# A Fourier mixer and an ELU feed-forward on one core: batch 1's twelve weight groups by three products in place of four

## The chip, the cores and the metric

The kernel runs on one core of one Trainium2 chip. The metric is the device time of one execution in microseconds (us); where several runs are shown, their median is taken. TensorE (PE in the profile) multiplies matrices, VectorE (DVE), ScalarE (ACT) and GpSimd (POOL) work element by element, and SyncE (SP) issues most of the transfers.

## The reference

```python
X = rfft(x, axis=1)                       # x: 8 batches x 3008 positions x 256
Yr = Xr @ w_r - Xi @ w_i + b_r
Yi = Xr @ w_i + Xi @ w_r + b_i
Y = sign(Y) * max(|Y| - 0.01, 0)          # real and imaginary part apart
y = irfft(Y, n=3008, axis=1)
h = y.reshape(24064, 256) @ moe_w_in      # 256 x 2048
g = where(h > 0, h, exp(min(h, 0)) - 1)
out = g @ moe_w_out                       # 2048 x 256
```

## The kernel before, in words

The transform over 3008 = 47 x 64 positions is done as small matrix products in five kinds of units. **A** transforms over 47 positions, **X** over 64 and leaves the spectrum in the tile `XT` with the real part (c=0) beside the imaginary part (c=1), for two halves of the 256 features (dt=0 and 1). **M** applies the weights `w_r` and `w_i` to 128 frequencies at a time, adds the bias and shrinks by 0.01. **B** and **Y** transform back; Y's result is `yT`, the input of the feed-forward. Between A and X, M and B, B and Y the data are turned through DRAM or SBUF by transfers: `DA` into `Z` (`load_Z`, line 223), `Y` into `Yx` (`turn_Y`, line 434), `DB` into `Bs` (`load_Bs`, line 476).

The feed-forward is a chain of 376 steps, 47 for each batch, in the main loop (line 1317). Step i multiplies 512 positions by 256 of the 2048 inner columns (`front`, line 1096: four matmuls of 512 columns into two banks of a pool of four, `hps`), turns the result into the ELU and multiplies that of step i-2 by `moe_w_out` (`back`, line 1174: eight matmuls of 256 columns). The ELU is exp on ScalarE, a clamp, and one last instruction on VectorE for each half (`finish_elu`, line 1153), which is issued a step later and frees the `hps` banks that `front` takes two steps later. The clamp (`elu`, line 1165) is done in one of three ways: on GpSimd (two instructions, line 1169), on VectorE (one of 128x1024, line 1171), or not at all, where ScalarE takes a Relu ahead of the exp (lines 1128 and 1133; steps with an M unit).

`plan(b)` (line 1222) lays the units of the next batch over the 47 steps of batch b: `f0[t]` holds what is issued ahead of step t's `front`, `f1[t]` what is issued behind it. Each engine runs its instructions in the order in which they are issued. For batch 1, prepared while batch 0 is worked on, the units start at step 10 (`FILL`): X0 to X7 in steps 10 to 17, M in 18 to 23, 25, 26, 28, 29, 31 and 32, B in 24, 27, 30 and 33 to 35, then the A and Y units. The six transfers that fill `Z` for batch 1 are issued in step 5: first three for the slots 0 to 7, then three for the slots 8 to 31. X unit (g, dt) reads the slots 8g to 8g+7.

There are two forms of M. Batches 0 and 1 use `m_group` (line 283): four matmuls of 128x512, one VectorE addition of the bias (line 302), and on GpSimd a clip (line 314) and a subtraction (line 315). Batches 2 to 7 use three real products (lines 317 to 350): six matmuls of 128x256, (Xr+Xi) w_r, Xi times -(w_i + w_r), and Xr times (w_i - w_r), two VectorE additions (lines 340, 341), and on GpSimd a further bias addition (line 346), the clip (349) and the subtraction (350). These need `sum_XT` (line 255; three GpSimd additions for each dt, in tiles `XS` and `busy`) and the weights as `three_weights` (line 272) makes them, five GpSimd instructions in steps 47 to 50.

The M groups of `m_group` take two banks from the pool that the X and B units use (`psF`, one tile of two banks), the three products two single banks of `psM`; changing between the two pools makes the new one wait for what the old one still holds. A B unit reads what `turn_Y` has moved of both M groups with its number; `turn_Y` for the last pair of batch 1 issues two of its four transfers from GpSimd's queue (line 438).

Of the kernel before, what the change touches and what calls it, by code (L numbers as in the profile page):

```python
# [8 lines left out]
ALU = mybir.AluOpType  # L9
# [20 lines left out]
def kernel(  # L30
# [11 lines left out]
    nc = tc.nc  # L42
    P = nc.NUM_PARTITIONS

    B, S, D = x.shape
# [5 lines left out]
    LAM = 0.01  # L51
# [44 lines left out]
    PER = S * NPAIR // TB  # L96
# [8 lines left out]
    Y_of = {}  # L105
# [17 lines left out]
    def unit_ps(name, alone):  # L123
        if alone:
            return pre2.tile([P, 2, 512], F32, name=name, tag="pre2")
        return last_banks("psF").tile([P, 2, 512], F32, name=name, tag="fps")
# [100 lines left out]
        nc.sync.dma_start(Z[a:P:4, s0:s1, :], dv[rows * a : rows * a + rows, s0:s1, :])  # L227

    def unit_X(b, u, alone=False, on_dve=False, apart=False):
        g, dt = (u // 2, u % 2) if b == 1 else (u % 4, u // 4)  # L230
        if u == 0:
            XT_of[b] = xtp.tile([P, 2, 2, K1 * N2], BF16, name="XT", tag="XT")
        XT = XT_of[b]
        if apart:
            psv = [t[:].rearrange("p (k j) -> p k j", j=P) for t in two_banks(pre1, "mps1")]
        else:
            ps = unit_ps("xps", alone)
            psv = [ps[:].rearrange("p a (k j) -> p (a k) j", j=P)]
        nk = 8 // len(psv)
        for kk in range(8):  # L240
            k = 8 * g + kk
            nc.tensor.matmul(  # L242
                psv[kk // nk][:, kk % nk, 0 : 4 * K1],
                lhsT=Z[:, k, dt * P : dt * P + P],
                rhs=M2[:, k].rearrange("p c m -> p (c m)"), start=True, stop=True,
            )
        for h, v in enumerate(psv):
            k0 = 8 * g + nk * h
            evac(
                XT[:, dt].rearrange("p c (m s) -> p c m s", s=NS)[:, :, :, k0 : k0 + nk],  # L250
                v[:, :, 0 : 4 * K1].rearrange("p k (c m) -> p c m k", c=2),
                on_dve and not h if apart else on_dve,
            )
# [24 lines left out]
            b_r_, b_i_ = (bias_bc[:, D * k : D * k + D] for k in range(2))  # L278
            nc.gpsimd.tensor_tensor(b_i_, b_i_, b_r_, ALU.subtract)

    mps_of = {}

    def m_group(b, q, i, ps, biased=False):
        XT = XT_of[b]
        o = (2 * q + i) * P
# [21 lines left out]
        return yb, clip  # L307

    def unit_M(b, q, i):
        if b == 1:  # L310
            if i == 0:
                mps_of[q] = unit_ps("mps", False)
            yb, clip = m_group(b, q, i, mps_of[q][:, i, :])
            nc.gpsimd.tensor_scalar(clip[:], yb, LAM, -LAM, ALU.min, ALU.max)
            nc.gpsimd.tensor_tensor(Y_of[b, q][:, i, :], yb, clip[:], ALU.subtract)
            return
        XT, o = XT_of[b], (2 * q + i) * P
        if i == 0:
            Y_of[b, q] = wk4.tile([P, 2, 2 * D], BF16, name="Y", tag="Y")
        ps, k1 = (  # L320
            last_banks("psM").tile([P, 2 * D], F32, name="mps", tag="mps") for _ in range(2)
        )
        ch, oc = divmod(o, 512)
        r, s = wcat_r, wcat_s
        todo = [
            (k1[:, 0:D], None, r[:, :, 0:D]),
            (ps[:, 0:D], XT[:, :, 1, o : o + P], s[:, :, 0:D]),
            (ps[:, D : 2 * D], XT[:, :, 0, o : o + P], s[:, :, D : 2 * D]),
        ]
        if o == 0 and b > 3:  # L330
            todo.append(todo.pop(0))
        for out_, lhs, w in todo:
            for dt in range(2):
                nc.tensor.matmul(  # L334
                    out_, lhsT=lhs[:, dt] if lhs is not None else sum_of(dt, ch)[:, oc : oc + P],
                    rhs=w[:, dt, :], start=(dt == 0), stop=(dt == 1),
                )
        yb = wk3.tile([P, 2 * D], F32, name="yb", tag="yb")
        clip = wk2.tile([P, 2 * D], F32, name="clip", tag="clip")
        nc.vector.tensor_tensor(yb[:, D : 2 * D], k1[:, 0:D], bias_bc[:, 0:D], ALU.add)  # L340
        nc.vector.tensor_tensor(  # L341
            yb[:].rearrange("p (c d) -> p c d", c=2),
            ps[:].rearrange("p (c d) -> p c d", c=2),
            yb[:, D : 2 * D].unsqueeze(1).to_broadcast([P, 2, D]), ALU.add,
        )
        nc.gpsimd.tensor_tensor(  # L346
            yb[:, D : 2 * D], yb[:, D : 2 * D], bias_bc[:, D : 2 * D], ALU.add
        )
        nc.gpsimd.tensor_scalar(clip[:], yb[:], LAM, -LAM, ALU.min, ALU.max)  # L349
        nc.gpsimd.tensor_tensor(Y_of[b, q][:, i, :], yb[:], clip[:], ALU.subtract)  # L350

    held = []

# [726 lines left out]
    FILL = 10  # L1080
# [141 lines left out]
    def plan(b):  # L1222

        f0 = [[] for _ in range(PER)]
        f1 = [[] for _ in range(PER)]
        mode = [None] * PER
        n1, n2 = b + 1, b + 2
# [6 lines left out]
        if n1 < B:  # L1234
            if b:
                lead, xs = 0, (3, 6, 9)
# [24 lines left out]
        for t, u in enumerate(seq, lead):  # L1261
            if u is None:
                continue
            if b and n1 < B:
                mode[t] = "act" if u in on_act or u[0] == "M" else "pool"
            if mode[t] == "act" and u[0] != "M":
                k = {"y": "Y"}.get(u[0], u[0])
                c = {"y": b, "A": n2}.get(u[0], n1)
                if c < B:
                    dve = (False, True) if k == "B" else (k != "X" or b < 3 and u[1] == 7,)  # L1270
                    f0[t].append(put(k, c, u[1], False, *dve))
            elif u[0] == "y":
                f0[t].append(put("Y", b, u[1]))
            elif u[0] == "n":
                f0[t].append(put("Y", n1, u[1]))
            elif u[0] == "A":
                if n2 < B:
                    f0[t].append(put("A", n2, u[1]))
            elif b == 0 and u == ("B", 5):
                f0[t].append(put("B", n1, 5, False, True))  # L1280
            else:
                f0[t].append(put(u[0], n1, *u[1:]))
            if u[0] == "M" and u[2] == 1:
                f1[t].append((turn_Y, (n1, u[1])))
            if u == ("B", 5):
                for w, k in enumerate((0, 2, 3, 4)):
                    f1[t + k].append((load_Bs, (n1, w, 0, 4 * K1 - 16 * (b == w == 0))))
            if u == ("A", 5) and n2 < B:
                for part in ((0, 8), (8, NS)):
                    f1[t] += [(load_Z, (n2, a, *part)) for a in range(3)]  # L1290
# [13 lines left out]
        if n2 < B:  # L1304
            for ci in range(3):
                f1[xs[ci]].append((load_x, (n2, ci)))
        if b and n1 < B:
            f0[seq.index(("X", 4))].append((sum_XT, (n1, 0)))
            f0[seq.index(("X", 7))].append((sum_XT, (n1, 1, range(2 if b < 3 else 3))))
            if b < 3:  # L1310
                f0[seq.index(("M", 2, 0))].insert(0, (sum_XT, (n1, 1, (2,))))
# [5 lines left out]
    for i in range(n + LAG):  # L1317
        if i == FILL:
            few.close()
        if i == LAG:  # L1320
            back(0, False)
        if early_h:
            h, on_act = early_h, False
        elif i < n:
            r = i % PER
            if r == 0:
                f0, f1, mode = plan(i // PER)
                used = [bool(u0 or u1) for u0, u1 in zip(f0, f1)]
            free = not used[r]
            bare = bare + 1 if free else 0  # L1330
            calm = free and (i >= n - 2 or (r + 2 < PER and not used[r + 1] and not used[r + 2]))
            for f, a in f0[r]:
                f(*a)
            if mode[r]:
                on_act = mode[r] == "act"
                pooled = not on_act
            else:
                on_act = any(f is unit_M for f, a in f0[r])
                pooled = free or i < FILL
            third = calm and bare % 3 == (2 if i // PER == B - 1 else 1)  # L1340
            h = front(i, third, on_act)
        finish_elu()
        if i < n:
            for f, a in f1[r]:
                f(*a)
            split = i > LAG and (i - LAG) % NPAIR == NPAIR - 1
            if split:
                back(i - LAG, True)
            elu(i, *h, pooled, on_act)
            if PER <= i < PER + 4:  # L1350
                three_weights(*divmod(i - PER, 2))
            if 1 <= i < 5:
                if i < 3:
                    scale_w_in(2, True, i - 1)
                scale_w_in(3, False, (i - 1) // 2, (i - 1) % 2)
            if i == n - 2:
                early_h = front(n - 1, True, False)
            elif early_h:
                early_h = None
        else:  # L1360
            split = False
        if i > LAG and not split:
            back(i - LAG, False)
# [30 lines left out]
```

## Time and profile before

| | |
|---|---|
| median of 3 runs | 872.06 us (871.14 to 872.1) |
| profiled execution | 871.1 us |
| its span in the trace | 869.3 us |
| granted TensorE clock | 0.999 of full speed |
| TensorE busy | 860.8 us, 99% |
| VectorE, ScalarE, GpSimd busy | 666.2, 715.4, 592.8 us |

The span runs from the first to the last instruction on the core; 1.8 us of the execution lie around it. A busy TensorE is not one at its peak, as the ends of its matmuls are modelled and overlap. The chain of waits says more: it is followed back from the last instruction, at each step to what released it. Rows of a timeline give the start, the time taken, engine, line and operation, and in brackets the idle time before with what ended it; neighbours of one kind are merged, with their number at the end.

### The profile page before, as it was taken

The numbers are of one execution on the slowest core, as the hardware profiler recorded it, in microseconds if no ns is written. First come the engines' busy times: TensorE is split into PE (matmuls) and PEld (weight loads), VectorE is DVE, ScalarE is ACT, GpSimd is POOL, SyncE is SP. The second block draws the span as 40 slices with busy tenths as digits, with TensorE's granted clock in tenths as the row PEclk, the third lists the DMA queues.
The fourth block names the chain that finished last, engine by engine and source line by source line (L and its number), as shares of the span: only waits on it lengthen the run. The fifth ranks groups of instructions, "written<-read, shape, count | busy, mean of one in ns | idle before, by whom it ended". The sixth has DMA issues, their size and how long they took to land.

```text
span 869.3 us, 18553 instructions
## 1 busy us (share of the span) xinstructions
PE 860.8 (99%) x6773; PEld 675.8 (78%) x6773; DVE 666.2 (77%) x1103; ACT 715.4 (82%) x1255; POOL 592.8 (68%) x866
## 2 busy tenths in 40 slices
PE   8999999999999999999999999999999999999997
PEld 6567677887788877887778877787877888787776
DVE  8889779697676886778866787677777687788775
ACT  8878888888978889798887988879887888876664
POOL 8671651898657986588846987459874697734664
PEclk9999999999999999999999999999999999999999
DMA  8897446532575135653365432753337313250111
GB/s 248 282 288 213 117 131 193 164 117 73 141 224 170 51 79 168 191 170 92 89 183 172 128 104 78 217 165 107 94 96 213 90 39 85 79 141 25 40 36 49
DMA packets 113597, 116.11 MB, mean 134 GB/s; under 512 B 11569, under 2 KB 103473, under 8 KB 110145
## 3 DMA queue, kind: packets, MB, share of 16 engines
q1 hardware_dynamic: 108512, 86.74, 35.2%
q0 software_dynamic: 4704, 27.92, 9.8%
q8 instruction: 53, 0.87, 0.4%
q14 instruction: 40, 0.32, 0.1%
q10 hardware_dynamic: 288, 0.26, 0.1%
HBM read 53.28 MB, written 48.23 MB: 117 GB/s over the span
## 4 chain that ended last, share of the span: by engine, by line
PE 94%; POOL 2%; DVE 1%; DMA 1%; ACT 1%; issue 0%; DVEq 0%; POOLq 0%
PE ps_o L1192 39%; PE hps L1118 34%; PE mps L334 5%; PE xps L242 3%; PE mps L1118 2%; PE yps L615 2%; PE bps L451 2%; PE mps L292 2%; PE aps L194 2%; POOL Y L350 1%; DMA xt<-in_x_dram 1%; PE aps L186 0%; POOL yb L346 0%; POOL clip L349 0%; DVE gT L1159 0%
## 5 line engine op out<-in xcount | busy, mean ns | idle before, releaser
L1159 DVE SCALAR_TENSOR_TENSOR gT<-Et,hps 128x512 fp32r<-128x512 f32 x630 | 403.1, 682 | 137.0 <-POOL Et L1169 127.0
L1192 PE MATMUL ps_o<-w_out_r,gT 128*128 128x256 f32 x3008 | 477.2, 301 | 0.0
L1192 PEld LDWEIGHTS ps_o<-w_out_r,gT 128*128 128x128 f32 x3008 | 404.4, 189 | 48.0 <-DVE osb L1203 0.2
L1169 POOL TENSOR_SCALAR Et<-Et 128x512 f32<-128x512 f32 x482 | 287.3, 615 | 203.1 <-ACT Et L1130 201.6
L1118 PE MATMUL hps<-yT,w_in_s 128*128 128x512 bf16 (+7 forms) x1620 | 366.7, 353 | 0.3
L1130 ACT ACTIVATE Et<-hps 128x512 f32<-128x512 f32 x514 | 282.7, 610 | 41.7 <-PE hps L1118 38.6
L1118 PEld LDWEIGHTS <-w_in_s 128*128 128x128 bf16 x1728 | 144.1, 98 | 104.7 <-issue 13.1
L1128 ACT ACTIVATE Et<-hps 128x512 f32<-128x512 f32 x192 | 104.5, 597 | 42.0 <-PE hps L1118 41.6
L1133 ACT ACTIVATE Et<-Et 128x512 f32<-128x512 f32 x192 | 110.5, 632 | 0.0
L350 POOL TENSOR_TENSOR Y<-yb,clip 128x512 bf16<-128x512 f32 x72 | 92.7, 1287 | 6.0
L346 POOL TENSOR_TENSOR yb<-yb,bias_bc 128x256 f32<-128x256 f32 x72 | 53.2, 738 | 11.3 <-DVE yb L341 11.2
L150 ACT CAST XT<-xps 128x768 bf16<-128x768 f32 x57 | 45.8, 804 | 14.1 <-PE xps L242 13.9
L341 DVE TENSOR_TENSOR yb<-mps,yb 128x512 f32<-128x512 f32 x72 | 49.8, 692 | 7.2
L150 ACT CAST yT<-yps 128x752 bf16<-128x752 f32 x56 | 44.1, 787 | 13.7 <-PE yps L615 13.5
L1161 DVE SCALAR_TENSOR_TENSOR gT<-hps,Et 128x512 fp32r<-128x512 f32 x78 | 50.2, 686 | 3.3
L349 POOL TENSOR_SCALAR clip<-yb 128x512 f32<-128x512 f32 x72 | 44.1, 613 | 6.3
L150 ACT CAST A<-aps 128x1024 bf16<-128x1024 f32 x40 | 40.7, 1018 | 8.1 <-PE aps L194 5.0
L150 ACT CAST Bz<-bps 128x1024 bf16<-128x1024 f32 x41 | 41.6, 1014 | 5.3 <-PE bps L451 5.0
L340 DVE TENSOR_TENSOR yb<-mps,bias_bc 128x256 f32<-128x256 f32 x72 | 30.5, 424 | 17.5 <-PE mps L334 15.7
L334 PE MATMUL mps<-wcat_s,XT 128*128 128x256 bf16 x288 | 43.2, 273 | 0.0
L1203 DVE COPY osb<-ps_o 128x512 f32<-128x512 f32 x46 | 31.7, 690 | 5.4 <-PE ps_o L1192 3.4
L260 POOL TENSOR_TENSOR XS<-XT 128x512 bf16<-128x512 bf16 x30 | 34.1, 1157 | 2.4 <-ACT XT L150 1.4
(216 smaller groups left out, 673.3 us busy)
## 6 DMA issues: line engine op xcount, KB each, us to landing
xt<-in_x_dram POOLq DMA_DIRECT2D x21, 1024.0 KB, 5.3
out_dram<-osb SPq DMA_DIRECT2D x154, 128.0 KB
Bs<-DB SPq DMA_DIRECT2D x30, 384.0 KB
Yx<-Y SPq DMA_DIRECT2D x166, 64.0 KB
DA<-A SPq DMA_DIRECT2D x19, 512.0 KB
DB<-Bz SPq DMA_DIRECT2D x19, 512.0 KB
Z<-DA SPq DMA_DIRECT2D x21, 384.0 KB
xt<-in_x_dram POOLq DMA_DIRECT2D x6, 512.0 KB, 6.2
```

The costliest lines, as they stand in the source:

```text
L150: nc.scalar.copy(dst, src)
L334: nc.tensor.matmul(out_, lhsT=lhs[:, dt] if lhs is not None else sum_of(dt, ch)[:, oc : oc + P], rhs=w[:, dt, :], start=(dt == 0), stop=(d ...
L346: nc.gpsimd.tensor_tensor(yb[:, D : 2 * D], yb[:, D : 2 * D], bias_bc[:, D : 2 * D], ALU.add)
L350: nc.gpsimd.tensor_tensor(Y_of[b, q][:, i, :], yb[:], clip[:], ALU.subtract)
L1118: nc.tensor.matmul(hps[s][:, c0:c1], lhsT=w_in_s[:, dt, ft * P : ft * P + P], rhs=yT_of[b][:, dt, t0 : t0 + c1 - c0], start=(dt == 0), sto ...
L1128: nc.scalar.activation(Et[:, s], hps[s], AF.Relu, scale=-1.0)
L1130: nc.scalar.activation(Et[:, s], hps[s], AF.Exp)
L1133: nc.scalar.activation(Et[:, s], Et[:, s], AF.Exp, scale=-1.0)
L1159: nc.vector.scalar_tensor_tensor(o, e, -1.0, h, ALU.add, ALU.max)
L1161: nc.vector.scalar_tensor_tensor(o, h, 0.0, e, ALU.max, ALU.add)
L1169: nc.gpsimd.tensor_scalar(e, e, 1.0, 0.0, ALU.min, ALU.max)
L1192: nc.tensor.matmul(po[q][:, j, :], lhsT=gT[:, s, i_ * P : i_ * P + P], rhs=w_out_r[:, ft, :], start=(ft == 0 and j == 0), stop=(ft == NFT ...
```

## The change

Batch 1's M groups go to the three products. The order of batch 1's X units becomes that of the others: X0 to X3 are dt=0 with g=0 to 3, X4 to X7 dt=1 (before: g=0 with dt=0 and 1, then g=1, and so on). `sum_XT` for dt=0 is issued in step 14 and for dt=1 in step 17, three instructions each. `three_weights` moves from steps 47 to 50 to steps 10 to 13. In the steps of B0, B1 and B2 the clamp of the ELU goes from VectorE to GpSimd. For the last M group (q=5, i=1) the subtraction goes from GpSimd to VectorE, issued behind that step's ELU instructions and ahead of `turn_Y`. The first group computes the product with the sums last.

```diff
     def unit_X(b, u, alone=False, on_dve=False, apart=False):
-        g, dt = (u // 2, u % 2) if b == 1 else (u % 4, u // 4)
+        g, dt = u % 4, u // 4
...
     def unit_M(b, q, i):
-        if b == 1:
-            if i == 0:
-                mps_of[q] = unit_ps("mps", False)
-            yb, clip = m_group(b, q, i, mps_of[q][:, i, :])
-            nc.gpsimd.tensor_scalar(clip[:], yb, LAM, -LAM, ALU.min, ALU.max)
-            nc.gpsimd.tensor_tensor(Y_of[b, q][:, i, :], yb, clip[:], ALU.subtract)
-            return
...
-        if o == 0 and b > 3:
+        if o == 0 and (b == 1 or b > 3):
             todo.append(todo.pop(0))
...
-        nc.gpsimd.tensor_tensor(Y_of[b, q][:, i, :], yb[:], clip[:], ALU.subtract)
+        if (b, q, i) == (1, 5, 1):
+            late_Y.append((Y_of[b, q][:, i, :], yb, clip))
+        else:
+            nc.gpsimd.tensor_tensor(Y_of[b, q][:, i, :], yb[:], clip[:], ALU.subtract)
+
+    late_Y = []
+
+    def finish_Y():
+        Y, yb, clip = late_Y.pop()
+        nc.vector.tensor_tensor(Y, yb[:], clip[:], ALU.subtract)
...
             if u[0] == "M" and u[2] == 1:
+                if (b, u[1]) == (0, 5):
+                    f1[t].append((finish_Y, ()))
                 f1[t].append((turn_Y, (n1, u[1])))
...
-        if b and n1 < B:
+        if b == 0:
+            f0[lead + 4].append((sum_XT, (n1, 0)))
+            f0[lead + 7].append((sum_XT, (n1, 1)))
+        elif n1 < B:
...
-                pooled = free or i < FILL
+                pooled = free or i < FILL or any(f is unit_B and a[1] < 3 for f, a in f0[r])
...
-            if PER <= i < PER + 4:
-                three_weights(*divmod(i - PER, 2))
+            if FILL <= i < FILL + 4:
+                three_weights(*divmod(i - FILL, 2))
```

More of the change, by code (lines that the diff above doesn't have):

```diff
@@ L279, in three_weights @@
             nc.gpsimd.tensor_tensor(b_i_, b_i_, b_r_, ALU.subtract)
-    mps_of = {}
     def m_group(b, q, i, ps, biased=False):
```

## The prediction

> **What bounds the kernel now.** I read the page first, then the chain of waits in the stretch that the change touches, then the timelines of GpSimd, VectorE and ScalarE there and in batch 2, which has the new form of M already.
>
> ```profile
> PE 860.8 (99%) x6773; PEld 675.8 (78%) x6773; DVE 666.2 (77%) x1103; ACT 715.4 (82%) x1255; POOL 592.8 (68%) x866
> PE 94%; POOL 2%; DVE 1%; DMA 1%; ACT 1%; issue 0%; DVEq 0%; POOLq 0%
> ```
>
> TensorE is the bound nearly everywhere. So an instruction less on it counts in full, and so does any wait that holds it. The chain through batch 1's units (start, length, what):
>
> ```profile
> 68.75 0.35 PE xps L242 x8
> ...
> 70.90 0.35 PE xps L242 x8
> ...
> 81.63 0.35 PE xps L242 x8
> ...
> 83.78 0.88 PE mps L292 x4
> ...
> 86.46 0.88 PE mps L292 x4
> ...
> 99.82 0.45 PE bps L451 x4
> ...
> 102.09 0.88 PE mps L292 x4
> ```
>
> X1 runs at 68.75, X2 at 70.90, X7 at 81.63, the first M group at 83.78, B0 at 99.82. An M step takes 2.68 us (83.78 to 86.46), a B step 2.27, and from 68.75 on TensorE waits for nothing.
>
> **Removed from TensorE.** Batch 2, in the chain around 198 us, shows both the price of the new group and, ahead of it, what GpSimd's lag does:
>
> ```profile
> 197.51 0.59 POOL Et L1169
> ...
> 198.12 0.70 DVE gT L1159
> ...
> 198.87 0.59 PE hps L1118 x2
> ...
> 200.97 0.67 PE mps L334 x6
> 201.65 0.43 PE hps L1118 x2
> ```
>
> Six matmuls of 256 columns take 0.67 where four of 512 took 0.88. Twelve groups: 12 x 0.21 = 2.52 us less. This is all that the change can gain on the path; an M step becomes 2.46.
>
> **X1's new wait.** X1 becomes (g=1, dt=0) and reads the slots 8 to 15, which come with the second three `Z` transfers. Before, X2 was the first to read them. GpSimd's gate waits for the same transfers:
>
> ```profile
> 57.61 7.52 SPq L227 DMA_DIRECT2D Z<-DA  x6
> ```
> ```profile
> 70.48 0.19 POOL L976 CAST gate<-Z 128x1 f32<-128x1 bf16 x1 [4.07 <-DMA Z<-DA]
> ```
>
> All six are issued by 65.13, and the gate sat idle for 4.07 us until they had landed, at about 70.45. Nothing in the change moves them. X2 at 70.90 just found them there; X1 at 68.75 must wait: 70.48 - 68.75 = 1.73 us in which TensorE has nothing else, as its queue is in order and step 11's `front` stands behind X1. The lower bound is 0, were the landing early. Beyond 1.73 I see nothing. I take 1.73. The other engines only catch up in it.
>
> **GpSimd becomes the path from X7 to B5.** Before, its part of a group was clip and subtraction:
>
> ```profile
> 85.68 0.61 POOL L314 TENSOR_SCALAR clip<-yb 128x512 f32<-128x512 f32 x1 [13.28 <-DVE yb L302]
> 86.37 1.27 POOL L315 TENSOR_TENSOR Y<-yb,clip 128x512 bf16<-128x512 f32 x1
> 87.59 0.59 POOL L121 DMA_DIRECT2D xt<-in_x_dram  x1
> ```
>
> That is 1.9 us in a step of 2.68. In batch 2, with sums of three ahead:
>
> ```profile
> 167.00 3.41 POOL L260 TENSOR_TENSOR XS<-XT 128x512 bf16<-128x512 bf16 x3
> ...
> 171.00 1.20 POOL L1169 TENSOR_SCALAR Et<-Et 128x512 f32<-128x512 f32 x2
> ...
> 181.36 0.74 POOL L346 TENSOR_TENSOR yb<-yb,bias_bc 128x256 f32<-128x256 f32 x1
> 182.18 0.61 POOL L349 TENSOR_SCALAR clip<-yb 128x512 f32<-128x512 f32 x1
> 182.88 1.29 POOL L350 TENSOR_TENSOR Y<-yb,clip 128x512 bf16<-128x512 f32 x1
> 184.13 0.74 POOL L346 TENSOR_TENSOR yb<-yb,bias_bc 128x256 f32<-128x256 f32 x1
> ```
>
> A group now costs GpSimd 2.77 us (181.36 to 184.13) against TensorE's 2.46. I walk it through in the times of before; the 1.73 us come on top. X7's copy:
>
> ```profile
> 82.03 0.80 ACT L150 CAST XT<-xps 128x768 bf16<-128x768 f32 x1 [0.36 <-PE xps L242]
> ```
>
> It ends at 82.83, so the three sums of dt=1 run from 82.90 to 86.31 undisturbed. The first is done at 84.05; the first group needs it for its last product at 83.78 + 0.45 = 84.23 (two of three products), so TensorE doesn't wait there (by 0.1, and it could become a wait of some tenths). VectorE at that time:
>
> ```profile
> 82.50 1.29 DVE L1161 SCALAR_TENSOR_TENSOR gT<-hps,Et 128x512 fp32r<-128x512 f32 x2
> ...
> 84.30 0.68 DVE L1171 TENSOR_SCALAR Et<-Et 128x1024 f32<-128x1024 f32 x1
> 84.90 0.68 DVE L302 TENSOR_TENSOR yb<-mps,bias_bc 128x512 f32<-128x512 f32 x1
> ```
>
> Its clamp of 1024 elements in 0.68 us goes at twice the rate of its other instructions (512 in 0.68), and now falls into the sums. No row of before has this pair side by side; the nearest is around 49 us, where VectorE's scaling of weights, also a TENSOR_SCALAR from SBUF to SBUF, meets GpSimd:
>
> ```profile
> 49.33 1.05 DVE L971 TENSOR_SCALAR w_in_s<-w_in_f 128x512 bf16<-128x512 f32 x1
> ```
> ```profile
> 49.29 1.58 POOL L1169 TENSOR_SCALAR Et<-Et 128x512 f32<-128x512 f32 x2
> ```
> ```profile
> L971 DVE TENSOR_SCALAR w_in_s<-w_in_f x5: 615/1049/1070, 33.2 to 49.3; 128x512 bf16<-128x512 f32 x5
> ```
>
> GpSimd's pair takes 1.58 where 1.20 is usual (171.00), VectorE's one 1.05 where the shortest of its kind took 0.615: each seems to wait until the other's instruction has ended. Bounds: 0, if only these forms shut each other out, and a whole sum, 1.14, for VectorE each time. I take the exclusion as it stands: the clamp, ready at 84.30, starts with the end of the second sum near 85.15 and ends near 85.75 (0.8 late), and the third sum ends near 86.9 (0.55 late). The first group's two additions on VectorE follow. Their price:
>
> ```profile
> 177.29 0.42 DVE L340 TENSOR_TENSOR yb<-mps,bias_bc 128x256 f32<-128x256 f32 x1
> ...
> 179.76 0.42 DVE L340 TENSOR_TENSOR yb<-mps,bias_bc 128x256 f32<-128x256 f32 x1
> ```
>
> An M step holds VectorE for 2.47 us, no less than TensorE, so it doesn't regain what it has lost either. So the first group reaches GpSimd at about 87.1 (86.3 without the exclusion).
>
> [...]
>
> From 87.1: six groups, 16.6, and the `load_x` behind the first (0.6, above) bring GpSimd to 104.3. Only then does it reach B0's clamps: 0.6 for the first, then VectorE's 0.70 and two hand-overs, so that step 26's `front` gets its bank at 105.7. TensorE would be there at 83.78 + 6 x 2.46 + 2.27 + 2.46 + 0.67 = 103.94: 1.8 us late (1.0 without the exclusion). The rows of batch 2 quoted above show this wait on a smaller scale: GpSimd's clamp at 197.51, VectorE at 198.12, TensorE's `front` held until 198.87. Further from 104.3: the second clamp and B1's, B2's pairs with it 3 x 1.2 = 3.6, five groups 13.9, the last group's addition and clip 1.4: 123.2. GpSimd idles in between, as it then waits for TensorE's late steps; an estimate of 0.6, since steps 28 to 32 leave it about 0.2 each. VectorE's subtraction (0.7, as L341's 512 elements) ends at 124.6. Then the transfers to B5:
>
> ```profile
> 122.46 1.28 POOL L315 TENSOR_TENSOR Y<-yb,clip 128x512 bf16<-128x512 f32 x1
> 124.04 1.29 POOL L429 DMA_DIRECT2D Yx<-Y  x2 [0.30 <-POOL Y L315]
> ```
> ```profile
> 127.19 0.45 PE bps L451 x4
> ```
>
> Before, 3.45 us lay between the end of Y (123.74) and B5 (127.19), with no idle TensorE, so the need is 3.45 at most; I take 3.3. B5 then starts at 127.9, plus 1.73 is 129.6, against 127.19.
>
> **Edits with no price of their own.** `three_weights` in steps 10 to 13:
>
> ```profile
> 156.22 0.67 POOL L276 TENSOR_TENSOR wcat_s<-wcat_s,wcat_r 128x256 bf16<-128x256 bf16 x1
> 156.84 0.73 POOL L279 TENSOR_TENSOR bias_bc<-bias_bc 128x256 f32<-128x256 f32 x1
> ```
>
> Four of the first and one of the second, 3.4 us, fill GpSimd's idle time ahead of the gate (4.07) and behind it (it had nothing for 13.28 us up to 85.68, but for `load_x`). The sums of dt=0 in step 14 meet VectorE's clamps likewise, but there the ELU has time in hand: its last instruction ends at 82.50 + 1.29 less a step of 2.15 = 81.64, and the second half of step 17's `front`, which needs the bank, starts at 81.63 + 0.35 + 0.43 = 82.41, 0.7 later. Moving the last subtraction to VectorE saves the 1.28 - 0.69 = 0.6 that GpSimd would take longer. The clamps of B0 to B2 free VectorE of 0.69 in steps where it isn't late, and cost GpSimd 1.2 each. Taking `three_weights` out of steps 47 to 50 frees GpSimd where it bounds nothing: 0. Behind B5 all runs relative to it.
>
> **The sum.** TensorE saves 2.52 and loses 1.73 to `Z` and about 3.2 to GpSimd's chain: 129.6 - 127.19 = **+2.4 us**. On the profiled execution (871.1) that is 873.5; on the median (872.06), 1 us higher, 874.4. I forecast 874.0.
>
> **The rivals.**
> - No exclusion between sums and clamps: +1.6, 872.7 to 873.7. For it: no row has just this pair. Chance 0.2.
> - `Z` lands in time for X1, and only GpSimd's chain counts: 2.4 - 1.73 = +0.7, 871.8 to 872.8. Against it: the gate's 4.07. Chance 0.1.
> - The other side: GpSimd's lag never reaches TensorE, because a group there takes no longer than a step. Then -2.52 + 1.73 = -0.8 (870.3 to 871.3), and with `Z` in time -2.5 (868.6 to 869.5). It decides where GpSimd's group falls from 2.77 to 2.46. Against it: the wait at 198.87, after four groups and then two; here there are six in a row. Chance 0.1, of which 0.05 with `Z` in time.
> - The groups don't get shorter among these neighbours, or the sum is late for the first group by the whole of one: +3.5 to +4.9, 875 to 877. Against it: the 0.67. Chance 0.1.
>
> **How the numbers follow.** The forecast has 0.5. The range is 871.7 to 875.5: from `Z` in time to a walk that is 1 us short. A measurement of this kernel can tell about 0.2% from no change, 1.74 us. Slower by more: four fifths of the forecast (0.40), a third of the first rival (0.06) and the last one (0.1), 0.56. Faster by more: the third rival with `Z` in time, 0.05. Within: the rest, 0.39.
>
> **What would show it.** After's chain has X1 near 70.5 with a wait for `Z`; VectorE's L1171 in step 17 takes over 1 us; GpSimd is busy without a gap from the sums of step 17 to B0's clamps; step 26's `front` waits for VectorE behind GpSimd; B5 starts near 129.6, and behind it both traces run at the same distance. If X1 starts at 68.75, or GpSimd's groups come every 2.46, the forecast is wrong.

## The result and the profile after

| | before | changed |
|---|---|---|
| median, same chip | 871.45 us (12 runs, 870.85 to 872.27) | 874.16 us (12 runs, 872.73 to 876.31) |
| ratio | | 1.0030, 95% interval 1.0021 to 1.0039 |

The change makes the kernel 2.7 us slower; 2.4 was forecast on the profiled execution. The page of the changed kernel, TensorE's busy time and the chain that ended last by engine:

```profile
PE 856.4 (98%) x6694; PEld 679.6 (78%) x6797; DVE 670.7 (77%) x1113; ACT 716.0 (82%) x1255; POOL 612.6 (70%) x889
...
PE 83%; POOL 6%; DMA 4%; DVE 4%; issue 2%; ACT 1%; SPq 1%; DVEq 0%; POOLq 0%; ACTq 0%
```

TensorE is busy 4.4 us less (860.8 before; a rough figure, as 103 of its 6797 matmuls have no record there), and the chain leaves it for 17% of the span in place of 6%. Part of that 17% belongs to this one execution, the slowest of its 12. In the table of windows of the same profile (length, busy time of PE, PEld, DVE, ACT and POOL, then PEclk, the granted clock, and the transfers' share and GB/s) something stands that has nothing to do with batch 1:

```profile
22.00:24.00 2.00, 1.79 (x36) 1.68 (x33) 1.16 (x2) 1.56 (x3) 1.93 (x4) 0.83 1.08 337
24.00:26.00 2.00, 2.00 (x29) 2.00 (x27) 1.98 (x4) 1.18 (x2) 1.59 (x3) 0.50 0.99 342
26.00:28.00 2.00, 1.89 (x12) 0.95 (x11) 1.16 (x2) 1.62 (x3) 0.00 (x0) 0.81 1.09 406
```

From 23.3 to 26.7 TensorE ran at half clock, and X0 starts 2.0 us later than before (68.48 for 66.46). So the changed kernel was run once more, and below "the changed kernel" means that second profile, in which the clock stays at 1.00 and X0 starts at 66.31. What TensorE waited for between 64 and 136 us (total, times, longest) in it:

```profile
PE bps L451 <- DMA Yx<-Y: 1.3, 1, 1.3
PE xps L242 <- DMA Z<-DA: 0.6, 1, 0.6
PE hps L1118 <- DVE gT L1159: 0.6, 1, 0.6
PE mps L325 <- DVE yb L332: 0.4, 1, 0.4
PE hps L1118 <- DVE gT L1161: 0.2, 1, 0.2
PE xps L242 <- DVE yT L148: 0.2, 1, 0.2
```

The same view of the kernel before has the last row alone:

```profile
PE xps L242 <- DVE yT L148: 0.2, 1, 0.2
```

So five waits are new: for `Z`, for VectorE twice around step 19, for VectorE behind GpSimd in step 26, and for the last group's transfer at B5. How much each costs is read from where TensorE's units start, their first matmul counted from that of X0 (us; worked out from the matmuls of each trace):

| | X1 | M0 | M2 | B0 | B1 | B4 | B5 | A0 | A1 |
|---|---|---|---|---|---|---|---|---|---|
| before | 2.14 | 17.16 | 22.51 | 33.20 | 40.82 | 58.31 | 60.58 | 62.84 | 65.19 |
| changed | 2.93 | 18.02 | 23.82 | 33.72 | 42.27 | 59.27 | 63.10 | 65.52 | 67.83 |
| bias addition left out, X1 early, clamp of step 16 moved (below) | 2.14 | 17.21 | 22.15 | 32.07 | 39.30 | 56.04 | 59.39 | 61.75 | 64.07 |

The third row has no wait ahead of B5 and shows what an M step is worth: M0 to B4 takes 38.83 for 41.15, 2.3 us less. Against that row from M0 to B4, and against the row of before elsewhere, the changed kernel loses 0.9 to M0, 0.9 from M0 to M2 (5.80 for 4.94), 1.3 from B0 to B1, 0.3 from B1 to B4, 1.6 from B4 to B5 and 0.2 behind it: 5.0, less 2.3 is 2.7, which is the distance at A0 (65.52 - 62.84).

The chain of waits shows what stands behind each. First X1 (start, length, what):

```profile
63.83 5.28 DMA Z<-DA
69.11 0.14 issue
69.24 0.50 PE xps L242 x8
```

Then VectorE and GpSimd around the sums, in their timelines:

```profile
78.08 1.31 DVE L1171 TENSOR_SCALAR Et<-Et 128x1024 f32<-128x1024 f32 x1
...
85.28 1.17 DVE L1171 TENSOR_SCALAR Et<-Et 128x1024 f32<-128x1024 f32 x1
86.37 0.41 DVE L331 TENSOR_TENSOR yb<-mps,bias_bc 128x256 f32<-128x256 f32 x1
86.81 0.69 DVE L332 TENSOR_TENSOR yb<-mps,yb 128x512 f32<-128x512 f32 x1
...
88.62 0.41 DVE L331 TENSOR_TENSOR yb<-mps,bias_bc 128x256 f32<-128x256 f32 x1
...
90.94 0.42 DVE L331 TENSOR_TENSOR yb<-mps,bias_bc 128x256 f32<-128x256 f32 x1
```
```profile
83.62 2.27 POOL L260 TENSOR_TENSOR XS<-XT 128x512 bf16<-128x512 bf16 x2 [4.11 <-ACT XT L150]
85.86 1.61 POOL L260 TENSOR_TENSOR busy<-XT 128x512 bf16<-128x512 bf16 x1
87.65 0.73 POOL L337 TENSOR_TENSOR yb<-yb,bias_bc 128x256 f32<-128x256 f32 x1 [0.18 <-DVE yb L332]
...
91.00 0.76 POOL L337 TENSOR_TENSOR yb<-yb,bias_bc 128x256 f32<-128x256 f32 x1
...
93.79 0.74 POOL L337 TENSOR_TENSOR yb<-yb,bias_bc 128x256 f32<-128x256 f32 x1
...
104.87 1.19 POOL L1169 TENSOR_SCALAR Et<-Et 128x512 f32<-128x512 f32 x2
```

VectorE's clamp takes 1.17 and 1.31 where 0.68 is usual, the sum beside it 1.61 where 1.16 is. Late as it is, VectorE then takes 2.32 us for an M step (88.62 to 90.94), less than TensorE's 2.46, so it regains some of its lateness. From 87.65 GpSimd has no idle time until it reaches B0's clamps at 104.87; a group takes 2.79 (91.00 to 93.79). Step 26 in the chain:

```profile
104.90 0.59 POOL Et L1169
105.51 0.70 DVE gT L1159
106.21 0.04 issue
106.25 0.59 PE hps L1118 x2
106.85 0.59 PE hps L1118 x2
```

It is the row of three that batch 2 showed in the profile before (GpSimd's clamp, VectorE, `front`). And B5:

```profile
123.67 0.62 POOL clip L340
124.32 0.70 DVE Y L350
125.02 0.28 issue
125.31 4.06 DMA Yx<-Y
129.37 0.05 issue
129.41 0.39 PE bps L451 x2
```

### The profile page after: what moved, and what is told of

It is laid out like the page before. It is cut to its first block, busy times and chain, and to the rows that moved or that the text cites. A ratio compares the mean times of both kernels' runs of the same rounds, so it can differ in the third digit from the quotient of the medians.

```text
span 874.5 us, 18532 instructions
## 1 busy us (share of the span) xinstructions
PE 856.4 (98%) x6694; PEld 679.6 (78%) x6797; DVE 670.7 (77%) x1113; ACT 716.0 (82%) x1255; POOL 612.6 (70%) x889
## 4 chain that ended last, share of the span: by engine, by line
PE 83%; POOL 6%; DMA 4%; DVE 4%; issue 2%; ACT 1%; SPq 1%; DVEq 0%; POOLq 0%; ACTq 0%
PE ps_o L1192 35%; PE hps L1118 30%; PE mps L325 5%; PE xps L242 2%; POOL Y L344 2%; PE mps L1118 2%; PE yps L615 2%; PE aps L194 2%; PE bps L451 2%; POOL yb L337 1%; DVE gT L1159 1%; POOL clip L340 1%; DMA w_in_f<-in_moe_w_in_dram 1%; PE aps L186 1%; POOL Et L1169 1%
## 5 line engine op out<-in xcount | busy, mean ns | idle before, releaser
L1169 POOL TENSOR_SCALAR Et<-Et 128x512 f32<-128x512 f32 x488 | 291.7, 617 | 206.5 <-ACT Et L1130 205.0
L1118 PE MATMUL hps<-yT,w_in_s 128*128 128x512 bf16 (+6 forms) x1525 | 360.6, 351 | 6.2 <-DVE gT L1159 0.9
L344 POOL TENSOR_TENSOR Y<-yb,clip 128x512 bf16<-128x512 f32 x83 | 106.9, 1287 | 6.9
L337 POOL TENSOR_TENSOR yb<-yb,bias_bc 128x256 f32<-128x256 f32 x84 | 62.0, 738 | 11.9 <-DVE yb L332 11.8
L332 DVE TENSOR_TENSOR yb<-mps,yb 128x512 f32<-128x512 f32 x84 | 58.1, 692 | 8.4
L340 POOL TENSOR_SCALAR clip<-yb 128x512 f32<-128x512 f32 x84 | 51.7, 615 | 7.4
L331 DVE TENSOR_TENSOR yb<-mps,bias_bc 128x256 f32<-128x256 f32 x84 | 35.6, 423 | 20.3 <-PE mps L325 18.3
L325 PE MATMUL mps<-wcat_s,XT 128*128 128x256 bf16 x336 | 50.5, 273 | 0.3 <-DVE yb L332 0.3
L1161 DVE SCALAR_TENSOR_TENSOR gT<-hps,Et 128x512 fp32r<-128x512 f32 x72 | 46.4, 686 | 3.3
L260 POOL TENSOR_TENSOR XS<-XT 128x512 bf16<-128x512 bf16 x35 | 40.2, 1172 | 9.7 <-ACT XT L150 8.7
```

The costliest lines, as they stand in the source:

```text
L325: nc.tensor.matmul(out_, lhsT=lhs[:, dt] if lhs is not None else sum_of(dt, ch)[:, oc : oc + P], rhs=w[:, dt, :], start=(dt == 0), stop=(d ...
L337: nc.gpsimd.tensor_tensor(yb[:, D : 2 * D], yb[:, D : 2 * D], bias_bc[:, D : 2 * D], ALU.add)
L1118: nc.tensor.matmul(hps[s][:, c0:c1], lhsT=w_in_s[:, dt, ft * P : ft * P + P], rhs=yT_of[b][:, dt, t0 : t0 + c1 - c0], start=(dt == 0), sto ...
L1169: nc.gpsimd.tensor_scalar(e, e, 1.0, 0.0, ALU.min, ALU.max)
```

## The experiments

The theory: TensorE saves what the rows of batch 2 say, and three things eat it: X1's wait for `Z`; clamps and sums that shut each other out, which make VectorE late; and GpSimd, whose group is longer than a step. The rivals: that the saving is smaller than it looks; that only the number of GpSimd's groups counts, wherever its clamps stand; and, formed on the way, that VectorE is as full as GpSimd. Each ratio is against runs of the kernel before on the same chip, whose medians were 871.23 to 871.37. The ratios are not quotients of the two medians; they differ from these by up to 0.0011.

**The changed kernel again** (no edit).

> The changed kernel once more, for a second profile: in the first one every step of the stretch starts about 2 us late, and X1 waited for Z to 71.7. Theory (Z wait 1.7, GpSimd's chain 3.2, TensorE saves 2.5): +2.4 to +2.7 us against the kernel before (871.45), X1 held for 1.5 to 1.8 us, B5 at 129.6, step 26's front held for 1.5 to 2 us. Rival (most of the loss is a late transfer ahead of step 10, which the change has nothing to do with): the profile without the delay shows B5 within 1 us of 127.2 and the time is within 1 us of before.

874.64 us (873.71 to 875.86), ratio 1.0039 (1.0026 to 1.0052). It is the profile that is read above. B5 comes at 129.41 for the 129.6 expected; X1's wait is 0.8 for 1.5 to 1.8, and step 26's `front` is held for 0.64 for 1.5 to 2, as part of the lateness is met at M2.

**The order of X alone**, in the kernel before:

```diff
-        g, dt = (u // 2, u % 2) if b == 1 else (u % 4, u // 4)
+        g, dt = u % 4, u // 4
```

> The kernel before with batch 1's X units in the order of the others and nothing else. Theory: X1 reads the slots 8 to 15 and waits for Z until about 70.45: +1.7 us, 873.2. Rival (X1's wait is regained later, as the engines behind TensorE catch up in it): 0 to +0.5 us.

872.45 us, ratio 1.0015 (1.0006 to 1.0023). In its trace X1 starts 3.44 us behind X0 in place of 2.14, and A0 64.14 in place of 62.84: a wait of 1.3 us (1.7 was expected) that goes through to the end undiminished, as the rest of that kernel has no time to give back.

**X1 on slots that have landed.** X1 becomes (g=0, dt=1), and the sums of dt=0, whose last X unit is then X4, move a step:

```diff
-        g, dt = u % 4, u // 4
+        g, dt = ((0, 0), (0, 1), (1, 0), (2, 0), (3, 0), (1, 1), (2, 1), (3, 1))[u] if b == 1 else (u % 4, u // 4)
...
-            f0[lead + 4].append((sum_XT, (n1, 0)))
+            f0[lead + 5].append((sum_XT, (n1, 0)))
```

> The changed kernel with X1 as (g=0, dt=1), so that X2 is again the first to read the late slots; the sums of dt=0 go to step 15, as dt=0 is complete with X4. Theory: the wait of 1.7 us goes, 1.7 us less than the changed kernel, +0.7 to +1 against before. Rival (GpSimd's chain sets the time alone, and the wait for Z is hidden in it, since the chain begins with the sums of step 17): less than 0.5 us gained.

873.39 us, ratio 1.0016 (1.0007 to 1.0025). X1's wait is gone (2.16 us behind X0, M0 17.22), and the rest of the loss stands: M0 to M2 still takes 5.74, B0 to B1 8.52. Against the changed kernel the medians gain 1.25 us, less than the 1.7 expected and more than the rival's 0.5.

**No bias addition on GpSimd** in batch 1; its imaginary half then has `b_r` for a bias:

```diff
-        nc.gpsimd.tensor_tensor(
-            yb[:, D : 2 * D], yb[:, D : 2 * D], bias_bc[:, D : 2 * D], ALU.add
-        )
+        if b != 1:
+            nc.gpsimd.tensor_tensor(
+                yb[:, D : 2 * D], yb[:, D : 2 * D], bias_bc[:, D : 2 * D], ALU.add
+            )
```

> The changed kernel without GpSimd's bias addition in batch 1 (0.74 us in each of twelve groups; the imaginary half of that batch then has b_r for its bias where b_i belongs). Theory: GpSimd's group is 2.03 us, shorter than TensorE's step of 2.46, its chain no longer ends last, and most of the 3.2 us go: 2 to 3 us less than the changed kernel, -0.5 to +0.7 against before, with X1's wait left in it. Rival (VectorE, with 2.47 us in an M step and clamps that the sums hold up, is what TensorE waits for): less than 1 us gained.

872.25 us, ratio 1.0013 (1.0005 to 1.0022). A group is 1.95 us on GpSimd, and the wait of step 26 is gone: B0 to B1 takes 7.23 for the changed kernel's 8.55. What stays are X1's wait (0.97), that of M2 (M0 to M2 5.78) and 0.7 inside B5. The median is 0.9 above before, a little over the -0.5 to +0.7 expected.

**One clamp more on GpSimd.** With the slots as above, step 16's clamp goes to GpSimd, so that the sums of step 15 meet fewer clamps:

```diff
-                pooled = free or i < FILL or any(f is unit_B and a[1] < 3 for f, a in f0[r])
+                pooled = free or i < FILL or i == FILL + 6 or any(f is unit_B and a[1] < 3 for f, a in f0[r])
```

> The changed kernel with X1 reading slots 0 to 7 (no wait for Z), the sums of dt=0 in step 15, and the clamp of step 16 on GpSimd, so that fewer of VectorE's clamps meet sums. Against the run with the slots alone (1.6 us above before): if the clamps shut out by the sums make VectorE late at the third M group (0.8 us there), that wait goes; but if GpSimd's groups are what sets B5, the time hardly follows, and the wait comes back at step 26: 1.3 to 1.6 above before, 872.7 to 873.0. If VectorE's lateness is itself on the path to the end, 0.8 above, 872.2.

872.34 us, ratio 1.0012 (1.0004 to 1.0021). M0 to M2 takes 4.95: VectorE is in time, so its lateness there did come from the clamps of the steps before. But B0 to B1 now takes 9.18 and B4 to B5 3.46. Of the 0.79 us given at M2, 0.66 are taken back at step 26, where GpSimd is as late as ever; the lateness is counted once, wherever TensorE meets it first. The ratio hardly moves (1.0016 to 1.0012, within both intervals).

**The same without the bias addition** (this edit and the one before together; the imaginary half has `b_r`).

> As the run before it, and GpSimd's addition of the imaginary half's bias is left out in batch 1, so that half has b_r for its bias; a group on GpSimd takes 1.95 us instead of 2.77. With the wait for Z, the shut-out clamps and GpSimd's lag all gone, what TensorE saves, 2.5 us, should be seen, less about 0.9 that B5 waits for the last group's longer way over VectorE, GpSimd and VectorE: 1.6 us under before, 869.8. If the saving on TensorE is not what the rows say, or VectorE's 2.47 us for an M step binds, it stays at before's 871.4 or over.

870.08 us, ratio 0.9991 (0.9981 to 1.0001). It is the third row of the table: up to B4 TensorE has the whole 2.3 us, and B5 takes 1.1 of them (3.35 behind B4 in place of 2.27). By the time alone it can't be told from no change; but by its trace the saving is real, and the rival that it is smaller falls. GpSimd waits for VectorE here ahead of each of the last groups (0.39 to 0.51 us ahead of the last four in the run that leaves out the bias addition alone), so what B5 loses is not GpSimd's lag.

**B0's to B2's clamps back on VectorE**, in the changed kernel:

```diff
-                pooled = free or i < FILL or any(f is unit_B and a[1] < 3 for f, a in f0[r])
+                pooled = free or i < FILL
```

> The changed kernel with the minimum of the ELU in the steps of B0, B1 and B2 back on VectorE; all else as changed. If GpSimd's gapless queue holds step 26's second layer because the clamp stands in it, the wait of 1.3 us there goes, and GpSimd, rid of three pairs of 1.2 us, comes to the last group up to 1.5 us earlier: 0 to 1.2 us above the kernel before (871.4 to 872.7), in place of 2.7. If only the number of GpSimd's groups counts, or VectorE's clamp is shut out by GpSimd for as long, it stays 2.7 above, 874.

874.61 us, ratio 1.0040 (1.0028 to 1.0052): a miss, nothing is gained. B0 to B1 does fall, to 7.65, but B5 comes 4.64 us behind B4, for 3.83. VectorE around the last pair of groups, then GpSimd:

```profile
119.15 0.75 DVE L1171 TENSOR_SCALAR Et<-Et 128x1024 f32<-128x1024 f32 x1 [0.74 <-ACT Et L1130]
119.82 0.41 DVE L331 TENSOR_TENSOR yb<-mps,bias_bc 128x256 f32<-128x256 f32 x1
120.33 0.69 DVE L332 TENSOR_TENSOR yb<-mps,yb 128x512 f32<-128x512 f32 x1
120.94 1.28 DVE L1161 SCALAR_TENSOR_TENSOR gT<-hps,Et 128x512 fp32r<-128x512 f32 x2
```
```profile
121.10 0.73 POOL L337 TENSOR_TENSOR yb<-yb,bias_bc 128x256 f32<-128x256 f32 x1 [1.75 <-DVE yb L332]
```

The clamp now stands ahead of the two additions, and GpSimd, which has caught up by then, waits 1.75 us for VectorE and gives the delay on to B5. VectorE itself has time here: it idles 0.74 us ahead of the clamp, until ScalarE's exp is done. The forecast's sentence that the clamps "free VectorE of 0.69 in steps where it isn't late" is right as to the lateness, but leaves out that the next group's additions stand behind the clamp, and start later by about its length. So in this kernel both places for a clamp cost about the same, and the number of GpSimd's instructions alone doesn't set the time: with fewer of them the delay comes by way of VectorE. The windows of this profile show a second price:

```profile
130.00:132.00 2.00, 1.39 (x9) 0.83 (x9) 0.34 (x1) 0.58 (x2) 0.46 (x1) 0.97 1.00 278
132.00:134.00 2.00, 2.00 (x11) 1.91 (x10) 1.97 (x4) 1.10 (x3) 0.00 (x0) 0.50 0.36 123
134.00:136.00 2.00, 2.00 (x8) 0.94 (x8) 1.81 (x3) 0.94 (x2) 0.00 (x0) 0.67 0.82 233
```

Right behind B5's wait, 1.8 us by the waits, the clock is at one half for 3.4 us, and A1 comes 2.91 us behind A0, where the changed kernel has 2.31. This execution is the slowest of the run's five (876.35), at a mean clock of 0.997 for 0.999 to 1.0 in the others, so the median should hold little of this price.

**The last subtraction back on GpSimd**, in the changed kernel:

```diff
-        if (b, q, i) == (1, 5, 1):
+        if False:
...
-                if (b, u[1]) == (0, 5):
-                    f1[t].append((finish_Y, ()))
```

> The changed kernel with the last group's subtraction back on GpSimd, where it takes 1.28 us in place of VectorE's 0.69. If the path from GpSimd's last clip to B5 is what TensorE waits for, B5 comes later by the difference less what the hand-over and the place in VectorE's queue cost (0.65 us idle there now): between nothing and 0.6 us over the changed kernel, 874.1 to 874.8. If the move to VectorE had no part in it, or cost time there, it is 0 to 0.5 under, 873.6 to 874.1.

875.91 us, ratio 1.0043 (1.0030 to 1.0056); the interval holds the changed kernel's 1.0039, so the times alone don't tell them apart. The median is above both forecasts; three of the six executions have a mean granted clock of 0.997, and they are the three slowest (876.37 to 876.61). In the trace the transfer is issued 59.69 us behind X0 in place of 59.00, so the move to VectorE is worth its 0.6 to 0.7. This profile, too, has the clock at one half for 3.4 us behind B5.

**A0 ahead of B5**, in the changed kernel:

```diff
-            ("M", 5, 0), ("M", 5, 1), ("B", 3), ("B", 4), ("B", 5), ("A", 0),
+            ("M", 5, 0), ("M", 5, 1), ("B", 3), ("B", 4), ("A", 0), ("B", 5),
```

> The changed kernel with A0 ahead of B5, nothing else: the last group's transfer has a step of 2.3 us more before B5 needs it. If B5's wait for the transfer behind the lagging GpSimd is 1.6 us of the 2.7 us lost, it goes: 1.1 us above the kernel before, 872.4. If VectorE, at 2.47 us a step, is what is late by then, the same time is lost in the steps after: 2.7 above, 874.

872.64 us, ratio 1.0011 (1.0002 to 1.0019). B4, A0, B5 follow each other in 2.34 and 2.29 us, and the last wait is gone for nothing. By the medians, 1.4 of the 2.7 us lost are left.

**All of these, clamps of B0 to B2 on VectorE.** X1 on landed slots, step 16's clamp on GpSimd, A0 ahead of B5, and the clamps as in the kernel before.

> All of the work is done. The changed kernel with X1 on slots 0 to 7 and the sums of dt=0 in step 15, step 16's clamp on GpSimd, the clamps of B0 to B2 back on VectorE, and A0 ahead of B5, so that the last group has a step more. If the three waits named (Z, GpSimd's clamp in step 26, B5) are all that ate the 2.5 us, this is 1 to 2 us under before, 869.4 to 870.4. If GpSimd's 2.77 us for a group binds by itself, the waits come back elsewhere and it is 0 to 1.5 above, 871.4 to 872.9.

871.12 us, ratio 1.0002 (0.9993 to 1.0011): no difference from before, and just under the second range. B0 to B1 takes 8.11, as VectorE, with a clamp and a copy ahead of the next additions, is late for B1.

**All of these, clamps on GpSimd, and five bias additions on TensorE.** The edits of the run before, but with B0's to B2's clamps on GpSimd as the change has them; and for the odd groups but the last, TensorE adds the bias with the identity matrix, ahead of the product (`bias_d`: the difference of the biases as bf16):

```diff
+        fold = b == 1 and i == 1 and q < 5
...
+            biased = fold and out_ is todo_i
+            if biased:
+                nc.tensor.matmul(out_, lhsT=idm[:], rhs=bias_d[:], start=True, stop=False)
...
-                    rhs=w[:, dt, :], start=(dt == 0), stop=(dt == 1),
+                    rhs=w[:, dt, :], start=(dt == 0 and not biased), stop=(dt == 1),
...
+        if not fold:
             nc.gpsimd.tensor_tensor(
```

> All of the work is done. X1 on slots 0 to 7, sums of dt=0 in step 15, step 16's clamp and those of B0 to B2 on GpSimd, A0 ahead of B5, and for five of the twelve groups TensorE adds the bias of the imaginary half (one more matmul of 256 columns, 0.11 us by the rows) in place of GpSimd's 0.73. Without any bias on GpSimd and with B5's wait still in it this was 1.2 us under the kernel before; the wait of 1.1 goes, five matmuls come, 0.55: if a group of 1.95 beside one of 2.77 is short enough for GpSimd, 1.2 to 1.8 under, 869.6 to 870.2. If VectorE's full steps bind, as in the run with the clamps back on VectorE, it is no faster than before, 871.3.

869.54 us (12 runs, 869.1 to 872.23) against 871.23, ratio 0.9981 (0.9971 to 0.9991). It does the whole work and beats both kernels. GpSimd in its timeline; an even group starts at 86.68, the next odd one at 90.06:

```profile
86.68 0.73 POOL L344 TENSOR_TENSOR yb<-yb,bias_bc 128x256 f32<-128x256 f32 x1
...
90.06 0.63 POOL L347 TENSOR_SCALAR clip<-yb 128x512 f32<-128x512 f32 x1
...
92.02 0.72 POOL L344 TENSOR_TENSOR yb<-yb,bias_bc 128x256 f32<-128x256 f32 x1
...
96.73 0.73 POOL L344 TENSOR_TENSOR yb<-yb,bias_bc 128x256 f32<-128x256 f32 x1
...
101.46 1.19 POOL L1176 TENSOR_SCALAR Et<-Et 128x512 f32<-128x512 f32 x2
```

Two groups take 4.71 us (92.02 to 96.73) beside two steps of TensorE, 5.04, and B0's clamps come at 101.46 for 104.87. The waits of TensorE between 64 and 136 us, and the chain by engine:

```profile
PE xps L242 <- DVE yT L148: 0.2, 1, 0.2
```
```profile
PE 97%; DVE 1%; DMA 1%; issue 0%; ACT 0%; POOL 0%; DVEq 0%; POOLq 0%
```

No wait is left but the one that the kernel before has too, and A1 comes 1.9 us earlier than there (63.26 behind X0 for 65.19), which is 2.3 less five matmuls of about 0.1.

## Why the prediction was right, and where its steps were not

1. **TensorE's saving**: forecast 2.52, shown 2.3 where nothing waits (0.19 for each group in place of 0.21).
2. **X1's wait for `Z`**: right in kind, too large: 0.8 in the profile read here (`Z` landed at 69.11, not at 70.45), 1.3 with the order alone. The 1.73 took the landing of one execution for fixed. In seven profiles with this order X1's wait lies between 0.8 and 1.55, each time less than the forecast.
3. **Clamps and sums shut each other out**: shown, in both directions (1.17 and 1.31 for 0.68, 1.61 for 1.16): the clamp of 85.28 ends at 86.45, 0.56 behind the end of the second sum (85.89), and the third sum ends 1.02 behind the clamp (87.47), both less than the 0.68 and the 1.16 that they take alone. GpSimd's first group starts 21.34 us behind X0, less the 0.79 of `Z` 20.55; forecast were 87.1 - 66.46 = 20.64. The walk without the exclusion, from which the rival has its +1.6, gives 86.3 - 66.46 = 19.84; so the trace agrees with the forecast's own, and that rival is out. What failed beside it is VectorE's price: the 2.47 us for an M step was the distance of two rows where VectorE keeps TensorE's pace. Where VectorE is late, an M step takes it 2.32, so it does regain lateness, against the forecast; the experiments' forecasts use the same 2.47.
4. **GpSimd's lag**: shown. It reaches B0's clamps 37.8 us behind X0 (38.56 - 0.79; forecast 104.3 - 66.46 = 37.84), and step 26's `front` gets its bank at 39.15 (forecast 39.24). The wait falls away when the group on GpSimd gets shorter (B0 to B1 7.23), and for the most part when GpSimd has no clamps there (7.65), but then VectorE is late at B5.
5. **Edits at no price**: two of five fail. The sums of dt=0 were to meet clamps with "0.7 in hand"; yet the chain runs on VectorE from 75.93 to 87.5, and M2 waits. The cure was in the run with step 16's clamp. That cost 0.9 us at M2, but of the lateness that step 26 would have met anyway: with the cure added to the landed slots, B0 to B1 went from 8.52 to 9.18. And moving the clamps of B0 to B2 gained nothing: on VectorE, where the next additions wait behind them, they cost about what they cost on GpSimd. The subtraction is worth its 0.6. The first group's sum is in time, as expected (M0 to M1 takes 2.50). That the moved `three_weights` cost nothing was not tested alone; TensorE shows no wait for it.
6. **The way to B5**: the last Y is ready where it was expected (57.92 behind X0 without the `Z` wait, forecast 124.6 - 66.46 = 58.14), but from there to B5's matmuls it takes 4.4 us (125.02 to 129.41), not 3.3 and not "3.45 at most". The last transfers, issued from GpSimd, before and then changed (count, size, median us to landing):

```profile
Yx<-Y POOLq DMA_DIRECT2D x2, 64.0 KB, 2.5
```
```profile
Yx<-Y POOLq DMA_DIRECT2D x2, 64.0 KB, 3.9
```

The sum came out right, +2.4 forecast for +2.7, partly by luck: `Z` took 0.9 us less than the 1.73 and the last transfers 1.1 more than the 3.3. The walk between the two, from GpSimd's first group to the last Y, held to 0.2 us. The median to landing of the last transfers is 2.3 in the last experiment and 4.2 in the third row of the table, where GpSimd is in time; so GpSimd's lag is not what makes them slow. What does was not tested: the first `DB<-Bz` that follows them on SP is issued 1.1 us behind in both traces.

The rivals: `Z` in time is out, as X1 waits in every profile with that order; a lag that never reaches TensorE is out for this kernel; groups that don't get shorter are out, as an M step takes TensorE 2.46 where nothing waits; that VectorE is as full as GpSimd is out too, as a late M step takes it 2.32. But that the lag "decides where GpSimd's group falls from 2.77 to 2.46" is what the last experiment uses.

## What to carry to other kernels

Work taken from the bound engine is worth its time only where the others' steps stay shorter than its own: here an M step was 2.46 us on TensorE, 2.32 on VectorE and 2.77 on GpSimd, and GpSimd's decided. An engine with time in hand still delays others by the order of its queue: VectorE's additions stood behind its clamps, and GpSimd waited 1.75 us for them. Look for who waits in a row of equal steps, not at busy shares (GpSimd was at 70%), and count a lateness once, at the first place where the bound engine meets it. The wait of a unit for a long way through three engines was cured here by putting a unit that needs nothing ahead of it (872.64 us with A0 ahead of B5, 874.64 without).

## What the runs showed of the hardware beside that

The view of waits can show less than TensorE loses. In step 26 it shows 0.6 us, but from there to B4 TensorE loses 1.6. Four matmuls of `front` take 1.19 us in place of 0.86, in that step and the next, at a granted clock of 1.00. Step 27 in the chain, VectorE's four instructions of `gT` at that time, and a `front` of the kernel before:

```profile
109.18 0.59 PE hps L1118 x2
...
109.77 0.59 PE hps L1118 x2
```
```profile
108.44 2.47 DVE L1159 SCALAR_TENSOR_TENSOR gT<-Et,hps 128x512 fp32r<-128x512 f32 x4
```
```profile
107.89 0.86 PE hps L1118 x4
```

Two matmuls fill one `hps` bank, and VectorE's `gT` frees the banks one at a time. The first two of its instructions here end at 109.12 and 109.72, and the pairs of matmuls start about 0.05 us behind each; in step 26 the ends are 106.20 and 106.80, and the pairs start at 106.25 and 106.85. So in both steps TensorE goes at VectorE's pace, 0.60 us for a bank where two matmuls need 0.43, which makes 0.33 us more for each step. The wait for the second bank hardly shows, because the modelled ends of the matmuls before reach up to it (109.18 and 0.59 make 109.77). The pairs start 0.60 apart in both steps of the changed kernel's first profile, too (108.73 and 109.33, 111.65 and 112.25), and with X1 on landed slots (106.81 and 107.41, 109.73 and 110.33).

The second is the clock. In two profiles that wait longer at B5 (1.8 us at a stretch with the clamps on VectorE; 1.9 us in two pieces with the subtraction on GpSimd) it was at one half for 3.4 us right behind it; behind the 1.3 us of the changed kernel's second profile it was not. Ahead of it TensorE was not idle all the time: in the run with the clamps on VectorE it was busy for 0.80 us of 128 to 130 and 1.39 of 130 to 132. In the changed kernel's second profile it was busy for 0.64 of 128 to 130, and the clock stayed at 1.00. Whether idle time halves it, and how much of it that takes, is not shown.
